# An attention and two expert layers on one core: float32r zero products, at changing addresses, in the idle places of the first batch

## The chip, the core and the metric

The kernel runs on one core of a Trainium2 chip, as one program in one launch. The metric is the device time of that core in microseconds (us). Five engines work side by side, each through its own queue of instructions: TensorE (PE) multiplies matrices, VectorE (DVE), ScalarE (ACT) and GpSimd (POOL) work on elements, and SyncE (SP) starts the transfers between the chip's memory and the core's.

## The reference

Three layers follow each other. The output of the attention is laid out as 4608 tokens of 512 values, and is the input of the first expert layer, whose output is the input of the second.

```python
def _attn_ref(q, k, v):                      # 8 batches, 8 heads, 576 positions, 64 values
    k_p = k.reshape(B, H, 72, 8, D).mean(axis=3)
    v_p = v.reshape(B, H, 72, 8, D).mean(axis=3)
    scores = scale * np.matmul(q, k_p.transpose(0, 1, 3, 2))
    scores = scores - np.max(scores, axis=-1, keepdims=True)
    attn = np.exp(scores)
    attn = attn / (np.sum(attn, axis=-1, keepdims=True) + 1e-09)
    return np.matmul(attn, v_p)

def _moe_ref(x, w_in, w_out):                # 4608 x 512, 512 x 2048, 2048 x 512
    h = x @ w_in
    return (h * np.cos(h)) @ w_out

def _moe2_ref(x, w_in, w_out):               # the same sizes
    h = x @ w_in
    return (h * np.clip(h + 3.0, 0.0, 6.0) / 6.0) @ w_out
```

## The kernel before

**The attention** goes batch by batch, and each batch in five query units of 128, 128, 128, 128 and 64 positions. `unit_s` (products at L490 or L494, all through `pe`) multiplies a unit's queries `qT` with the pooled keys, four heads a half; the keys stand block by block in `kbd`, a pair of tiles whose other places are zero. In batch 0 each half's maximum is taken on DVE (`mx`, L521) and the exponential on ACT with its sum (L531); in later batches DVE subtracts the maximum (`e`, L524) and ACT takes one exponential for the unit (L541). `unit_norm` turns the sum into a reciprocal on DVE (`sm`, L549 to L551), scales `e` with it on POOL (L553) and copies the rest of the heads aside (L555). `unit_pt` turns `e` over by products with the identity matrix `ident` and ACT copies the result to `pf` (L587); `unit_pt_rest` does that for the rest (L608). `pv` multiplies `pf` with the pooled values `vmf` and `vrf` into a 128 x 256 output. In batch 0 ACT copies that output, rounded to float32r, to `xh` (L641), and DVE subtracts `xh` from the output and keeps the difference in `xl` (L642): so the expert layer's input stands in two parts.

**Around it**: `pool_k` sums eight neighbouring key positions on DVE (`pk`, L428, two instructions), from `raw_k`, which SP loads; `pool_v` does that for the values (`vt`, L442, two instructions). `convert_weights` unpacks the expert weights from 64-bit words: its steps are L126, L130, L135 and L138 on DVE, squares and copies on ACT and a difference on POOL (L143, L144). `fill` (L500) puts four bf16 products with the identity ahead of the scores of batch 1 and six ahead of its first output product.

**The first expert layer** multiplies float32r parts: three products stand for one in full precision. The products with the first matrix have line L301 (output `h`), those with the second L344 (output `y`); between them lie the cosine on ACT and DVE. From the end of batch 0 on, expert steps and pieces of the attention alternate on PE until the attention's last batch. The second expert layer (L1021) follows at the end, by blocks of seven products in place of eight.

**What sets the order.** A scheduler with costs of its own puts each engine's instructions in a row, from the program in the order it was written. In batch 0 `front` (L712) writes PE's order by hand: each product that goes through `pe` is tied behind the one ahead of it (`issue_after`) while `in_order` is not empty. The other engines' orders, and PE's after `in_order.clear()`, are the scheduler's.

**The idle places.** `front` calls `keep_busy` (L703) eight times, with the counts of `KB` (L710). Its products multiply a part of `kbd[1]`, which is zero then and is read as bf16, with itself; 128 columns of it are the weights, 512 the moving operand. The result goes to `y2`, a tile in PSUM, and nothing reads it. The first count, 20, comes ahead of the first scores. This text calls the seven other calls groups 1 to 7. Group 1 stands between the second unit's scores and the third's, group 2 behind the third's, groups 3 to 5 around the second and third turning over and the fourth unit's scores, group 6 behind the third unit's turning over, and group 7 behind the fourth's. Then come the last output products of that part and the free order.

The outputs of `pv` in batch 0 use `y2` and `y3` in turn, in the same PSUM as the zero products: `piece("v")` takes `y2` for the first and third of four output products and `y3` for the second and fourth. An output must have been read by L641 and L642 before the next product that is written to its place starts.

Of the kernel before, what the change touches and what calls it, by code (L numbers as in the profile page):

```python
# [9 lines left out]
F32R = mybir.dt.float32r  # L10
# [14 lines left out]
def f(ap):  # L25
    return ap.bitcast(F32)
# [3 lines left out]
def tile_kernel(ctx, tc, q, k, v, wi1, wo1, wi2, wo2, ident_d, mask_d, out):  # L30
    nc = tc.nc
# [3 lines left out]
    P = 128  # L35
    N = 512
# [44 lines left out]
    pool_a = ctx.enter_context(tc.tile_pool(name="pool_a", bufs=1))  # L81
# [317 lines left out]
    def load_kv(b, nm):  # L399
        if nm == "v":  # L400
            src = v[b]
            pairs = src.rearrange("(j x) e -> x j e", x=2 * SP)
            for half in range(2):
                o = half * NP * VR
                nc.sync.dma_start(
                    out=raw_t[o : o + NP * VR, NP, :],
                    in_=src.rearrange("(j x) e -> j x e", x=2 * SP)[:, P:],
                )
            nc.sync.dma_start(out=raw_t[:, :NP, :], in_=pairs[:P])
            return  # L410
        nc.sync.dma_start(out=raw_k, in_=k[b])
# [75 lines left out]
    def pe(fn, *args, **kw):  # L487

        if not in_order:
            return fn(*args, **kw)  # L490
        with ExitStack() as order:
            if in_order[-1] is not None:
                order.enter_context(tc.issue_after(in_order[-1].ins))
            in_order.append(fn(*args, **kw))  # L494
# [48 lines left out]
    def unit_norm(n):  # L543
        w = UNITS[n % NU][1]
        e = ebuf[n % NE][:w, : H * SP].rearrange("p (h s) -> p h s", s=SP)
        sm = sums.pop(n, None)
        if sm is None:
            sm = ap.tile([P, H, 4], F32, tag="sm", name="sm", bufs=3)[:, :, 0:1]
            nc.vector.tensor_reduce(out=sm[:w, :, 0], in_=e, op=ALU.add, axis=AX.X)  # L549
        nc.vector.tensor_scalar(out=sm[:w], in0=sm[:w], scalar1=1e-9, scalar2=None, op0=ALU.add)  # L550
        nc.vector.reciprocal(out=sm[:w], in_=sm[:w])  # L551
        eng = nc.vector if n in ND else nc.gpsimd
        eng.tensor_tensor(out=e, in0=e, in1=sm[:w].to_broadcast([w, H, SP]), op=ALU.mult)  # L553
        e = ebuf[n % NE][:w]
        eng.tensor_copy(  # L555
            out=e[:, H * SP :].rearrange("p (t j x) -> p t j x", t=2, x=VR),
            in_=pairs_of(e)[:, :, P:].unsqueeze(1).to_broadcast([w, 2, NP, VR]),
        )
# [95 lines left out]
    def attention():  # L654
# [5 lines left out]
        for n in range(NU, units + 3):  # L660
# [21 lines left out]
            while finished < normed and n - finished >= 2:  # L682
# [12 lines left out]
                if qi == NU - 1:  # L695
                    done.append(qb)
                    if qb + 1 < B:
                        pool_v(qb + 1)
                        make_v(qb + 1)
                        if qb + 2 < B:  # L700
                            load_kv(qb + 2, "k")

    def keep_busy(n):  # L703

        z = kbd[1].rearrange("p j x -> p (j x)").bitcast(BF16)
        ps = ps_y.tile([P, N], F32, tag="y2", name="y2")
        for _ in range(n):
            pe(nc.tensor.matmul, ps, z[:, :P], z[:, :N], start=True, stop=True)

    KB = [20, 7, 9, 3, 4, 3, 3, 4]  # L710

    def front():  # L712

# [14 lines left out]
        w_convert(3)  # L728
        in_order.append(None)
        keep_busy(KB[0])  # L730

        def s(n):
            unit_s(n, 0)
            unit_s(n, 1)

        s(0)
        load_q(4)
        s(1)
        keep_busy(KB[1])
        unit_norm(0)  # L740
        s(2)
        unit_norm(1)
        keep_busy(KB[2])
        unit_pt(0)
        keep_busy(KB[3])
        s(3)
        pool_v(0)
        make_v(0)
        load_kv(1, "k")
        keep_busy(KB[4])  # L750
        unit_pt(1)
        unit_pt_rest(0, 0)
        unit_norm(2)
        w_convert(1)
        keep_busy(KB[5])
        for j in range(NP):
# [31 lines left out]
    for bl in range(NB):  # L788
        n = NAL[bl]
        steps += [(0, (0, bl), bl, fc, fc == 0, fc == n - 1) for fc in range(n)]  # L790
    SA = len(steps)
    for bl in range(NB):
        n = NAL[bl]
# [35 lines left out]
    def w_convert(n=3):  # L829
        nonlocal converted  # L830
        m, fc, hf, home = wjobs[converted]
        converted += 1
        running.extend(convert_weights(m, fc, hf))
        w_ops(n)
# [336 lines left out]
    for step, pb in enumerate(ORDER2):  # L1171
        t0, w = PAIRS[pb]
# [10 lines left out]
        for n in range(7):  # L1183
            for q in range(4):
                at = ring[turns2 % 3]
# [64 lines left out]
```

## Time and profile before

| | |
|---|---|
| median of three runs | 1657.24 us (1656.57 to 1657.41) |
| the profiled execution, its own time | 1657.06 us |
| its span, first to last instruction | 1655.3 us |
| mean granted clock of TensorE | 0.998 |
| busy: PE, DVE, ACT, POOL | 1635.6, 1107.3, 892.7, 313.4 us |
| share of the chain that ended last: PE, DVE, DMA, ACT | 94%, 3%, 1%, 1% |

The profile is that of one execution, and its times start at the first instruction. The time of a run is 1.76 us longer than the span. Busy times are sums over an engine's instructions, and say how full an engine is, not whether its time counts: for that one looks at a stretch, and at what ended each wait in it. PEclk is the clock that PE was granted, 1.00 for 2.4 GHz and 0.50 for 1.2 GHz; PEld are PE's weight loads, which run beside its products; DMA is the busy share of the 16 DMA engines and GB/s what they moved. A row of a timeline joins instructions of one kind that follow each other, and gives the start of the first. A float32r product is shown as f32 in the rows.

### The profile page before, as it was taken

The page shows a single profiled execution, that of the slowest core. Times are in us where ns is not written, and L with a number is a line of the kernel's source. Part 1 is how long each engine was busy: PE and PEld are TensorE (multiplying, and loading weights), DVE is VectorE, ACT ScalarE, POOL GpSimd, SP SyncE. Part 2 cuts the span into 40 slices and gives each one's busy share as a digit, 9 for nine tenths or more (in the row PEclk, how much of TensorE's full clock was granted, in tenths as well). Part 3 has the DMA queues.
Part 4 walks back from the last instruction along what each step waited for, and adds up shares of the span by engine and source line. Part 5 has one row for each costly group of instructions (what it writes and reads, how often), then busy time and mean ns, then how long its engine had stood idle before and what let it go on. Part 6 is the DMA issues. An engine that isn't in the chain of part 4 may idle for free.

```text
span 1655.3 us, 21211 instructions
## 1 busy us (share of the span) xinstructions
PE 1635.6 (99%) x7725; PEld 1343.0 (81%) x7727; DVE 1107.3 (67%) x1522; ACT 892.7 (54%) x1328; POOL 313.4 (19%) x257
## 2 busy tenths in 40 slices
PE   8999999999999999999999999999999999999999
PEld 4666788888888888888888898888878888888889
DVE  7998466665676778887776444545364676767665
ACT  6687687776555555555555333435353444444444
POOL 5466343232332111001114002022020000000000
PEclk9999999999999999999999999999999999999999
DMA  8687243124343575666653573242449944435130
GB/s 253 214 271 234 83 125 94 59 67 138 126 123 107 172 251 191 207 204 203 207 177 125 179 286 144 105 178 115 152 156 331 359 171 153 140 115 177 53 123 31
DMA packets 154760, 273.05 MB, mean 165 GB/s; under 512 B 16288, under 2 KB 79904, under 8 KB 153632
## 3 DMA queue, kind: packets, MB, share of 16 engines
q1 hardware_dynamic: 154656, 271.70, 49.1%
q8 instruction: 61, 1.00, 0.2%
q14 instruction: 43, 0.35, 0.1%
HBM read 166.79 MB, written 104.86 MB: 164 GB/s over the span
## 4 chain that ended last, share of the span: by engine, by line
PE 94%; DVE 3%; DMA 1%; issue 1%; ACT 1%; SPq 0%; POOL 0%; DVEq 0%; POOLq 0%; ACTq 0%
PE bank L1021 42%; PE h L301 23%; PE y L344 23%; PE ap_ps L490 6%; DMA raw_v<-in_v_dram 1%; DMA raw_k<-in_k_dram 1%; DVE pk L428 0%; DVE mx L521 0%; DVE vt L442 0%; DVE a L138 0%; PE ap_ps L500 0%; DVE e L524 0%; DVE a L126 0%; DVE sm L550 0%; DVE sm L549 0%
## 5 line engine op out<-in xcount | busy, mean ns | idle before, releaser
L1021 PE MATMUL bank<-wa,wb 128*128 128x512 f32 (+1 forms) x1368 | 287.7, 358 | 0.0
L1021 PEld LDWEIGHTS bank<-wa,wb 128*128 128x128 f32 x1368 | 231.2, 189 | 37.7
L344 PE MATMUL y<-gh,wb 128*128 128x512 f32 x648 | 210.9, 389 | 0.0
L301 PE MATMUL h<-xh,wb 128*128 128x512 f32 x648 | 206.6, 389 | 0.0
L883 ACT ACTIVATE wa<-wu 128x1024 fp32r<-128x1024 f32 (+1 forms) x130 | 127.3, 980 | 141.8 <-PE bank L1021 121.2
L1021 PE MATMUL bank<-wu,wb 128*128 128x512 f32 (+1 forms) x792 | 198.4, 386 | 0.0
L314 DVE SCALAR_TENSOR_TENSOR g<-h,t 128x512 f32<-128x512 f32 x144 | 99.1, 688 | 110.7 <-ACT t L309 110.0
L1021 PEld LDWEIGHTS bank<-wu,wb 128*128 128x128 f32 x792 | 148.8, 188 | 29.9
L344 PE MATMUL y<-gh,wa 128*128 128x512 f32 x504 | 170.0, 396 | 0.0
L301 PE MATMUL h<-xh,wa 128*128 128x512 f32 x504 | 165.8, 402 | 0.4 <-ACT xh L641 0.4
L275 POOL TENSOR_TENSOR xl<-xr,xh 128x512 fp32r<-128x512 f32 x68 | 94.9, 1412 | 325.9 <-ACT xh L274 277.8
L309 ACT ACTIVATE t<-h 128x512 int32<-128x512 f32 x144 | 85.4, 593 | 123.5 <-PE h L301 122.8
L317 ACT ACTIVATE g<-g,bias_c 128x512 f32<-128x512 f32 x144 | 104.2, 724 | 79.1 <-DVE g L314 78.3
L344 PEld LDWEIGHTS y<-gh,wb 128*128 128x128 f32 x648 | 121.7, 188 | 25.2
L301 PEld LDWEIGHTS h<-xh,wb 128*128 128x128 f32 x648 | 121.6, 188 | 25.2
L324 ACT ACTIVATE gh<-g 128x512 fp32r<-128x512 f32 x144 | 90.4, 628 | 68.1 <-DVE g L321 67.8
L884 DVE TENSOR_TENSOR wa<-wu,wa 128x1024 fp32r<-128x1024 f32 (+1 forms) x80 | 89.5, 1123 | 55.4 <-ACT wa L883 55.3
L344 PE MATMUL y<-gl,wb 128*128 128x512 f32 x324 | 126.0, 389 | 0.0
L301 PE MATMUL h<-xl,wb 128*128 128x512 f32 x324 | 122.6, 389 | 0.0
L321 DVE TENSOR_TENSOR g<-h,g 128x512 f32<-128x512 f32 x144 | 98.6, 685 | 32.4 <-ACT g L317 32.0
L1021 PE MATMUL bank<-wa,wa 128*128 128x512 f32 (+1 forms) x552 | 117.4, 359 | 0.0
L1139 ACT ACTIVATE wu<-bank,bias_c 128x1024 f32<-128x1024 f32 (+1 forms) x60 | 61.8, 1031 | 94.3 <-PE bank L1021 94.2
(176 smaller groups left out, 2873.9 us busy)
## 6 DMA issues: line engine op xcount, KB each, us to landing
g_d<-wu SPq DMA_DIRECT2D x64, 512.0 KB, 3.0
wu<-g_d SPq DMA_DIRECT2D x56, 512.0 KB, 4.4
wb<-s_d SPq DMA_DIRECT2D x36, 512.0 KB, 4.8
xr<-x_d SPq DMA_DIRECT2D x68, 256.0 KB, 3.3
s_d<-wa SPq DMA_DIRECT2D x32, 512.0 KB, 3.6
s_d<-wa SPq DMA_DIRECT2D x32, 384.0 KB, 3.0
raw_k<-in_k_dram SPq DMA_DIRECT2D x8, 1152.0 KB, 6.0
yp_d<-ys SPq DMA_DIRECT2D x36, 256.0 KB, 3.3
```

Of the source, the lines that this page charges most:

```text
L275: nc.gpsimd.tensor_tensor(out=xl, in0=t, in1=f(xh), op=ALU.subtract)
L301: nc.tensor.matmul(h, (wh, wl)[a][:, cs], xs_[key, c][z], start=(n == 0), stop=(n == 3 * NC - 1))
L309: nc.scalar.activation(out=t, in_=hs[s], func=AF.Copy, bias=0.25, scale=INV_2PI)
L314: mark[s] = nc.vector.scalar_tensor_tensor(out=g, in0=hs[s], scalar=INV_2PI, in1=t, op0=ALU.mult, op1=ALU.subtract)
L317: nc.scalar.activation(out=g, in_=g, func=AF.Sin, scale=TWO_PI, bias=bias_c[:, 1:2])
L321: nc.vector.tensor_tensor(out=g, in0=hs[s], in1=g, op=ALU.mult)
L324: nc.scalar.activation(out=gh, in_=g, func=AF.Copy)
L344: nc.tensor.matmul(y[c], a, z, start=(first and n == 0), stop=(last and n == 2))
L490: return fn(*args, **kw)
L883: nc.scalar.activation(out=hi, in_=src, func=AF.Copy)
L884: el.tensor_tensor(out=lo, in0=src, in1=f(hi), op=ALU.subtract)
L1021: nc.tensor.matmul(bank[:, e, :wide], w[:, j, h, e], z[:, j], start=start and j == 0 and x == 0, stop=stop and j == 1 and x == 2, skip_gro ...
```

## The change

The first 20 zero products stay as they are. Those of groups 1 to 7 read a tile of their own, `zeros`, which takes the slot `a13` of pool_a (a slot that holds weights later) and is set to zero by one instruction on POOL. They are float32r, and go through a list of 14 pairs of offsets, three products at each pair: the first number moves the moving operand, the second the weights, in elements of four bytes, so the two addresses take different values modulo 256 bytes. The counts of groups 1 to 7 go from 7, 9, 3, 4, 3, 3, 4 to 9, 9, 6, 3, 3, 6, 6, which is 33 before and 42 after. The lines behind the new code stand 17 further down.

```diff
@@ -700,14 +700,31 @@
                         if qb + 2 < B:
                             load_kv(qb + 2, "k")
 
+    PLACES = [
+        (0, 0), (0, 32), (0, 16), (0, 48), (32, 32), (32, 0), (16, 16),
+        (16, 0), (0, 8), (0, 56), (8, 8), (32, 48), (48, 48), (48, 32),
+    ]
+    zeros = pool_a.tile([P, 1024], F32R, tag="a13", name="wa13", bufs=1)
+    nc.gpsimd.memset(f(zeros), 0.0)
+    zeroed = []
+
     def keep_busy(n):
 
         z = kbd[1].rearrange("p j x -> p (j x)").bitcast(BF16)
         ps = ps_y.tile([P, N], F32, tag="y2", name="y2")
         for _ in range(n):
-            pe(nc.tensor.matmul, ps, z[:, :P], z[:, :N], start=True, stop=True)
-
-    KB = [20, 7, 9, 3, 4, 3, 3, 4]
+            zeroed.append(n)
+            if len(zeroed) <= KB[0]:
+                pe(nc.tensor.matmul, ps, z[:, :P], z[:, :N], start=True, stop=True)
+                continue
+            at, w = PLACES[(len(zeroed) - KB[0] - 1) // 3]
+            w += N
+            pe(
+                nc.tensor.matmul, ps, zeros[:, w : w + P], zeros[:, at : at + N],
+                start=True, stop=True,
+            )
+
+    KB = [20, 9, 9, 6, 3, 3, 6, 6]
 
     def front():
 
```

The scheduler counts the new products at costs of its own, and so writes other orders on all engines: on DVE, ACT and POOL in the stretch up to some 150 to 240 us, on PE up to some 600 us. From there on each engine's order is the same as before. Two places show what moves.

On DVE, in batch 0, around the first four output products of `pv`, before the change (`xl` is L642's difference of an output `y2` or `y3`, `pk` the keys' sum for batch 1, `sm` the fifth unit's sum, `a` and `e` belong to a weight's conversion; numbers behind a name tell tiles apart):

```order
L138 SCALAR_TENSOR_TENSOR a_313<-e_314,a_313 128x512
L642 TENSOR_TENSOR xl_326<-y2_322,xh_325 128x256
L428 TENSOR_REDUCE pk_425<-raw_k_107 128x144
L642 TENSOR_TENSOR xl_333<-y3_329,xh_332 128x256
L428 TENSOR_REDUCE pk_425<-raw_k_107 128x144
L642 TENSOR_TENSOR xl_340<-y2_336,xh_339 128x256
L550 TENSOR_SCALAR sm_411<-sm_411 64x8
L642 TENSOR_TENSOR xl_347<-y3_343,xh_346 128x256
L551 RECIPROCAL sm_411<-sm_411 64x8
L135 SCALAR_TENSOR_TENSOR a_477<-st_148,a_477 128x512
```

The same place after the change:

```order
L138 SCALAR_TENSOR_TENSOR a_319<-e_320,a_319 128x512
L428 TENSOR_REDUCE pk_436<-raw_k_107 128x144
L642 TENSOR_TENSOR xl_332<-y2_328,xh_331 128x256
L642 TENSOR_TENSOR xl_339<-y3_335,xh_338 128x256
L428 TENSOR_REDUCE pk_436<-raw_k_107 128x144
L550 TENSOR_SCALAR sm_422<-sm_422 64x8
L135 SCALAR_TENSOR_TENSOR a_488<-st_150,a_488 128x512
L642 TENSOR_TENSOR xl_346<-y2_342,xh_345 128x256
L642 TENSOR_TENSOR xl_353<-y3_349,xh_352 128x256
```

The first sum `pk` now stands ahead of the first subtraction and the second subtraction ahead of the second sum; L550 and L135, which stood behind the third subtraction, stand ahead of it. The third subtraction (from `y2`) is the one that must have read `y2` before group 6 may write there.

On PE, around the first turning over in batch 1, which started at 58.42 us before the change (`ident,e_104` and `ident,e_105` are the turnings over of its first and second unit, `kbd,qT` a unit's scores; rows of L301 and L344 are products of an expert step with the first and second matrix; the rows left out are four `fill` products):

```order
L344 MATMUL y_909<-gh,wa_138 128x512
L301 MATMUL h<-xh,wa_752 128x512 x4
L301 MATMUL h<-xl,wa_752 128x512 x4
L301 MATMUL h<-xh,wa_753 128x512
L490 MATMUL ap_ps<-ident,e_104 128x128 x4
...
L490 MATMUL ap_ps<-kbd_102,qT 128x144 x4
L301 MATMUL h<-xh,wa_753 128x512 x3
L490 MATMUL ap_ps<-ident,e_105 128x128 x4
```

The same place after the change (behind the second "..." six more rows of L344 are left out, and the last of the eight stands):

```order
L301 MATMUL h<-xl,wa_763 128x512
L301 MATMUL h<-xh,wa_764 128x512 x4
L344 MATMUL y_917<-gh,wa_139 128x512
L344 MATMUL y_917<-gl,wa_139 128x512
L344 MATMUL y_917<-gh,wa_140 128x512
L490 MATMUL ap_ps<-ident,e_104 128x128 x4
...
L490 MATMUL ap_ps<-kbd_102,qT 128x144 x4
L344 MATMUL y_918<-gh,wa_139 128x512
...
L344 MATMUL y_920<-gl,wa_139 128x512
L490 MATMUL ap_ps<-ident,e_105 128x128 x4
```

Three products of the second matrix stand ahead of that turning over in place of one with the first, and eight of the second matrix in place of three of the first ahead of the next one. The `fill` products that stood behind the second turning over still stand there.

## Rows read from the trace of the kernel before

**Rows 1.** Stretches: length, busy PE, PEld, DVE, ACT, POOL (instructions), PEclk, DMA, GB/s.

```profile
64.30:67.70 3.40, 2.94 (x12) 2.07 (x11) 3.40 (x6) 3.37 (x6) 2.12 (x2) 0.50 0.92 359
67.70:139.00 71.30, 70.71 (x326) 48.47 (x326) 65.72 (x111) 53.19 (x94) 42.64 (x39) 1.00 0.76 246
142.80:146.20 3.40, 3.40 (x11) 2.85 (x11) 1.47 (x3) 3.37 (x6) 2.52 (x3) 0.50 0.83 238
160.00:1655.30 1495.30, 1489.29 (x7037) 1242.45 (x7035) 967.54 (x1281) 775.87 (x1066) 224.24 (x167) 1.00 0.47 157
```

**Rows 2.** PE's timeline, 0 to 60 us: start, length, instructions, [idle before <- releaser].

```profile
11.29 1.67 PE L494 MATMUL y<-kbd 128*128 128x512 bf16 x7
12.80 0.65 PE L494 MATMUL ap_ps<-kbd,qT 128*128 128x144 f32 x4
14.34 0.76 PE L494 MATMUL h<-kbd,qT 128*128 128x144 f32 x4 [0.88 <-ACT e L531]
...
22.19 0.88 PE L494 MATMUL y<-ident,e 128*128 128x128 f32 x6 [1.66 <-POOL e L553]
...
31.46 0.81 PE L494 MATMUL y<-kbd 128*128 128x512 bf16 x2
...
34.03 0.33 PE L490 MATMUL y<-ident,e 64*128 64x64 f32 x2 [0.25 <-POOL e L553]
...
37.44 0.50 PE L301 MATMUL h<-xh,wa 128*128 128x512 f32 x1 [0.38 <-ACT xh L641]
37.77 0.41 PE L490 MATMUL ap_ps<-kbd,qT 128*128 128x144 f32 x2
```

**Rows 3.** PE's timeline, products of the first matrix in a row.

```profile
55.10 1.07 PE L301 MATMUL h<-xh,wa 128*128 128x512 f32 x4
56.01 1.07 PE L301 MATMUL h<-xl,wa 128*128 128x512 f32 x4
```

**Rows 4.** DVE's timeline, 25 to 35 us.

```profile
27.06 0.67 DVE L138 SCALAR_TENSOR_TENSOR a<-e,a 128x512 f32<-128x512 bf16 x1
...
27.99 1.33 DVE L428 TENSOR_REDUCE pk<-raw_k 128x144 f32<-128x1152 f32 x1
...
30.84 0.40 DVE L642 TENSOR_TENSOR xl<-y,xh 128x256 fp32r<-128x256 f32 x1
31.17 0.57 DVE L550 TENSOR_SCALAR sm<-sm 64x8 f32<-64x8 f32 x1
31.66 0.41 DVE L642 TENSOR_TENSOR xl<-y,xh 128x256 fp32r<-128x256 f32 x1
...
32.10 0.86 DVE L135 SCALAR_TENSOR_TENSOR a<-st,a 128x512 uint32<-128x512 uint32 x1
```

**Rows 5.** PE's timeline, the scores and turnings over behind batch 0.

```profile
51.19 0.65 PE L490 MATMUL ap_ps<-kbd,qT 128*128 128x144 f32 x4
...
58.42 0.66 PE L490 MATMUL ap_ps<-ident,e 128*128 128x128 f32 x4 [1.12 <-POOL e L553]
...
64.76 1.01 PE L500 MATMUL ap_ps<-ident 128*128 128x256 bf16 x4 [2.39 <-ACT pf L587]
...
141.57 0.63 PE L490 MATMUL ap_ps<-ident,e 128*128 128x128 f32 x4 [2.09 <-DVE e L524]
```

**Rows 6.** DVE's timeline, 56 to 107 us.

```profile
56.93 0.19 DVE L551 RECIPROCAL sm<-sm 128x8 f32<-128x8 f32 x1
...
69.56 0.18 DVE L551 RECIPROCAL sm<-sm 128x8 f32<-128x8 f32 x1
...
71.81 1.74 DVE L442 TENSOR_REDUCE vt<-raw_v 128x192 f32<-128x1536 f32 x1
...
106.53 1.35 DVE L428 TENSOR_REDUCE pk<-raw_k 128x144 f32<-128x1152 f32 x1 [2.05 <-DMA raw_k<-in_k_dram]
```

**Rows 7.** ACT's timeline, 62 to 65 us.

```profile
62.25 1.28 ACT L541 ACT_TABLE_LOAD   x1
...
64.13 0.58 ACT L587 ACTIVATE pf<-ap_ps 128x512 f32<-128x512 f32 x1
```

## The prediction

> **What bounds the kernel now.** I read the table by stretches first, to see which engine fills which part. From 160 us to the end TensorE (PE) is busy for 1489.29 of 1495.30 us [rows 1], and the change leaves every instruction there where it was; so the end comes as early as PE enters that part, and what PE loses or wins before 160 us goes through one to one. Second, the clock column of the same table: PE is granted half its clock in 64.3 to 67.7 us and in 142.8 to 146.2 us [rows 1], each time behind a wait of PE of more than 2 us (2.39 us before 64.76, 2.09 us before 141.57 [rows 5]). Half the clock over 3.4 us loses about 1.7 us of PE's work each time. Third, PE's timeline, for its waits and what the zero products cost. Fourth, VectorE's (DVE's): between 67.7 and 139 us it is busy for 65.72 of 71.30 us while PE is busy for 70.71 [rows 1]; here both are nearly full, and DVE has as much say as PE.
>
> **The zero products.** A bf16 product of 512 columns costs 0.216 us: seven take from 11.29 to 12.80 [rows 2]. Where float32r products follow each other, four take from 55.10 to 56.01, 0.227 us each [rows 3]. The first of a run costs more, because its weights are not loaded behind the work ahead: the one at 37.44 keeps the next back until 37.77, 0.33 us, so 0.11 us is exposed [rows 2]. A group of n then costs 0.227n + 0.11 us in place of 0.216n. The seven groups go from 7, 9, 3, 4, 3, 3, 4 (33 products, 7.1 us) to 9, 9, 6, 3, 3, 6, 6: 42 x 0.227 + 7 x 0.11 = 10.3 us, or 3.2 us more. Bounds: no row shows other pairs of addresses. Below, 0.216 (the bf16 row) would give 9.1 us; above, the dearest I can read is 0.33 for every one, 13.9 us. I take 0.227, the nearest row in type and size, and keep -1.2 and +3.6 us for the range. The measured 0.227 is what enters the sum. The Trainium skill's page "TensorE: Matmul & The Clock Gate", section "Back-to-back issue gap", gives one gap for 512 columns whatever the type, 518 cycles, some 0.216 us; by it the 42 products would be 0.5 us cheaper. The rows agree with that for bf16 and not for float32r.
>
> Most of this lies in time in which PE waited anyway. Group 1 grows by 0.64 us ahead of a wait of 0.88 us (14.34), groups 3 to 5 together by about 0.9 us around one of 1.66 us (22.19) [rows 2]: no cost, and if those covers were gone, 1.5 us. The memset of the operand is one instruction on GpSimd before anything waits for that engine: no cost.
>
> **The wait that the change adds.** Groups 6 and 7 do not hide. Group 6 writes y2, which must first be read by the xl subtraction (L642) of the third output product of this batch. In DVE's old order that is reached at 30.84 us, after xl, pk, xl, pk [rows 4]. In the new one the same four rows stand ahead of it in another order, and then L550 and L135 as well. By their lengths of 0.57 and 0.86 us, less the 0.08 us by which a row reaches into the next (31.17 to 31.66), it starts 1.2 us later, at about 32.1, and ends near 32.5. The group stood at about 31.46 before; it starts 1.0 us later, is 0.8 us longer, and group 7 is 0.6 us longer: 2.4 us. The waits of 0.25 us (34.03) and 0.38 us (37.44) [rows 2] go, so the first expert product comes about 1.8 us late, at 39.2 us. Behind it are queued all of PE's later instructions, and DVE's row maxima wait for those.
>
> **The order behind it.** Now the order matters more than the products. Before the transposes that start at 58.42 us PE used to run 33 products of the first matrix and 12 of the second; now 36 and 3, six fewer, 1.4 us. The fourth unit's scores stand behind ten more of them, 2.3 us. So PE, 1.8 us late, ends those scores near 51.7 + 1.8 + 2.1 = 55.6 us (51.7 is the old end; 0.2 us of exposed loads goes). The reciprocal of the first unit, which came at 56.93 [rows 6], now stands directly behind that unit's maximum and no longer behind the second pk: about 56.2. GpSimd's scaling takes the same 1.5 us from there as between 56.93 and 58.42: e is there at 57.7, when PE has just run five and three products more (55.6 + 1.9 = 57.5). The wait of 1.12 us [rows 5] shrinks to about 0.2.
>
> Next stands the wait of 2.39 us for pf [rows 5]. ScalarE came to pf at 64.13 behind a table load of 1.28 us at 62.25 and an exponential [rows 7]. It has the same two ahead of it now, but its earlier work ends sooner, since three expert steps no longer alternate in between; counted through, pf starts at about 62.4 and ends at 63.0. PE meanwhile runs eight products of the second matrix in place of three of the first and gets there at 62.3. So the four fillers start at about 63.05, not 64.76, with the same 48 expert products done: **PE is 1.7 us ahead**, the 3.2 us included. And these two waits are about 1 us together in place of 3.5, so I expect no drop of the clock there: another 1.7 us, **3.4 us in all at 68 us**.
>
> **What is late next.** DVE. At the reciprocal that stood at 69.56 us [rows 6] it would be 4.2 us early, of which 2.2 us is work put off (a vt reduction, a maximum, two subtractions): 2.0 us ahead. By the wait at 141.57 us one L138 more (0.67 us at 27.06, 0.6 without the reach into the next [rows 4]) stands behind and not ahead: 2.6 us. PE, 3.4 us ahead, then waits 0.8 us longer there, its clock falls a second time as before, and what remains is DVE's lead. **The sum: 1657.06 us (the profiled execution: its span of 1655.30 and 1.76 us around it; the median of the runs is 1657.24) - 2.6 = 1654.5 us.** The unknown product price, -1.2 to +3.6 us, is half hidden by the longer waits: about -0.6 to +1.8 on this.
>
> **Rivals.**
> 1. *More than I count.* DVE waited 2.05 us for raw_k at 106.53 [rows 6]. In the new order that load stands earlier in SP's queue, and DVE has 20 rows between the two pk pairs there, more than before. If that wait goes too, DVE is 4.6 us ahead at 141.57, PE waits about 1 us and keeps its clock: 2.6 + 2.0 + 1.7 = 6.3, **1650.8 us**. Against it: PE's products would have to be in step everywhere between.
> 2. *Slower.* In the new order both pk reductions of batch 4 (1.3 us each by the row at 27.99 [rows 4]), the longer vt reduction (1.66 us by the next start; 1.74 at 71.81 [rows 6]) and an L321 (about 0.6) stand ahead of the reciprocal that stood near 100 us: 4.8 us more work ahead of it. Against the lead of 2.0 us that unit comes 2.8 us later than before; PE, which is early, waits there, and its clock falls once more (1.7 us): +4.5, **1661.6 us**. It decides if DVE still stands at pk for raw_k, so that rival 1's 2 us are not won, and if PE has no other products ahead of those transposes.
> 3. *No gain.* The 1.8 us from batch 0 run through: the waits of 1.12 and 2.39 us are set by DVE's and ScalarE's chain, and if that starts as late as PE does, PE waits as long as before and its clock falls in the same two places. The change then adds zero products and nothing else: **1657.1 us**, up to 1658.9 if none of the 1.8 us hides.
>
> **How the numbers follow.** Forecast 0.45, rival 1 0.25, rival 2 0.15, rival 3 0.15. A measurement of this kernel can tell about 0.2% (3.3 us) from no change, so faster means under 1653.9 us and slower over 1660.6. The forecast's own range, 1652.5 to 1656.5, lies on both sides of the first bound: a third of it is faster. Faster 0.25 + 0.14 = 0.39, slower 0.14 (rival 2, of which a little falls short of the bound), the rest 0.47 is within. For 8 in 10 the range must hold the forecast, rival 3, most of rival 1 and the near part of rival 2: 1650.5 to 1660.0 us.
>
> **What would show it.** Right: float32r zero products 0.227 us apart with 0.11 us before the second; group 6 starting at 32 to 33 us behind xl; the first expert product at 39 us; the four fillers of 64.76 at about 63; no half clock near 64 us; a longer wait of PE near 137 us. Wrong: products at some addresses clearly over 0.24 us; pf no earlier than 64 us; a stretch of half clock anywhere between 40 and 130 us; PE waiting for e near 100 us. What I trust least is the count through DVE's and ScalarE's new order over 100 us, where one wait more moves the end by its length.

## The result, and the profile after

| | before | after | ratio, 95% interval |
|---|---|---|---|
| with the result | 1657.33 us, 4 runs | 1667.09 us (1664.75 to 1672.38), 4 runs | 1.0062 [1.005, 1.0074] |
| once more | 1657.82 us, 15 runs | 1665.0 us (1663.98 to 1669.63), 5 runs | 1.0046 [1.0032, 1.0059] |

The change makes the kernel about 0.5% slower, 7 to 10 us. The forecast was 1654.5 us in a range up to 1660.0, so the time lies outside it and on the other side.

The profiled execution took 1672.38 us, the slowest of its four runs. Two rows of its table by stretches, with the columns of [rows 1]:

```profile
40.00:57.00 17.00, 15.37 (x47) 11.16 (x46) 10.75 (x17) 4.57 (x10) 5.99 (x6) 0.60 0.46 149
...
160.00:1670.60 1510.60, 1504.44 (x7102) 1254.49 (x7101) 979.37 (x1301) 788.14 (x1083) 230.55 (x174) 1.00 0.47 157
```

From 160 us on PE is as full as before (idle for 6.2 us, against 6.0), so the loss lies ahead of that. The prediction's sentence that every instruction there stays where it was is too strong, since PE's order differs up to some 600 us; it does no harm to the sum. What is new is the clock: 0.60 in 40 to 57 us, where PE was at full clock before. Its PE timeline, with the columns of [rows 2]:

```profile
10.92 2.34 PE L494 MATMUL y<-wa 128*128 128x512 f32 x9
13.10 0.65 PE L494 MATMUL ap_ps<-kbd,qT 128*128 128x144 f32 x4
...
22.49 1.33 PE L494 MATMUL y<-ident,e 128*128 128x128 f32 x6 [1.94 <-POOL e L553]
...
42.02 0.70 PE L494 MATMUL y<-pf,vmf 128*128 128x256 f32 x2 [1.63 <-DVE xl L642]
```

The clock is half in 22.7 to 26.2, 43.2 to 56.9, 77.4 to 80.8 and 159.3 to 162.7 us, 23.9 us in all, against 6.8 before. On the page PE is busy for 1647.2 us in place of 1635.6 and idle for 23.4 in place of 19.7. So the 15.3 us between the two profiled executions are (23.9 - 6.8) / 2 = about 8.5 us of half clock, 3.2 us of zero products (the prediction's count) and 3.7 us of waits.

Most of the 8.5 us belongs to that execution: the four runs have mean granted clocks of 0.993, 0.998, 0.997 and 0.996 in the order of 1672.38, 1664.75, 1665.81 and 1668.36 us. A second profile of the same kernel (1665.0 us, clock 0.998 as before) has half clock for 6.8 us like before, and is the one to compare. PE's waits in it:

```profile
22.46 0.88 PE L494 MATMUL y<-ident,e 128*128 128x128 f32 x6 [1.94 <-POOL e L553]
...
29.22 0.70 PE L494 MATMUL y<-pf,vmf 128*128 128x256 f32 x2 [1.10 <-DVE xl L642]
...
32.14 1.64 PE L494 MATMUL y<-wa 128*128 128x512 f32 x6
...
38.71 0.50 PE L301 MATMUL h<-xh,wa 128*128 128x512 f32 x1
...
40.38 0.70 PE L494 MATMUL y<-pf,vmf 128*128 128x256 f32 x2 [0.93 <-DVE xl L642]
...
64.82 0.60 PE L500 MATMUL ap_ps<-ident 128*128 128x256 bf16 x4 [1.02 <-ACT pf L587]
...
69.42 0.63 PE L490 MATMUL ap_ps<-ident,e 128*128 128x128 f32 x4 [1.72 <-DVE e L524]
```
```profile
97.67 1.20 PE L301 MATMUL h<-xh,wa 128*128 128x512 f32 x4 [1.00 <-ACT wa L143]
...
106.37 0.97 PE L344 MATMUL y<-gh,wa 128*128 128x512 f32 x3 [0.71 <-ACT gh L324]
...
116.46 0.50 PE L301 MATMUL h<-xl,wa 128*128 128x512 f32 x1 [0.83 <-POOL xl L275]
...
146.16 0.63 PE L490 MATMUL ap_ps<-ident,e 128*128 128x128 f32 x4 [1.49 <-DVE e L524]
...
151.73 1.19 PE L490 MATMUL ap_ps<-kbd,qT 128*128 128x144 f32 x4 [2.48 <-DVE e L524]
```

Here PE is busy for 1639.8 us of 1663.2, so idle for 23.4 us. Of the 7.9 us that this span is longer, 3.7 are waits, 3.2 the products, and 1.0 is other time in which PE counts as busy. This tells what PE did and not what caused it: the crossed kernels below part that.

### The profile page after: what moved, and what is told of

Read it like the earlier page. It is cut to its first block, busy times and chain, and to the rows that moved or that the text cites. A ratio compares the mean times of both kernels' runs of the same rounds, so it can differ in the third digit from the quotient of the medians.

```text
span 1670.6 us, 21235 instructions
## 1 busy us (share of the span) xinstructions
PE 1647.2 (99%) x7736; PEld 1352.7 (81%) x7736; DVE 1113.2 (67%) x1522; ACT 891.1 (53%) x1326; POOL 312.8 (19%) x258
## 4 chain that ended last, share of the span: by engine, by line
PE 92%; DVE 4%; issue 1%; POOL 1%; ACT 1%; DMA 1%; SPq 0%; POOLq 0%; DVEq 0%; ACTq 0%
PE bank L1038 41%; PE h L301 22%; PE y L344 22%; PE ap_ps L490 5%; DMA raw_v<-in_v_dram 1%; DVE a L138 1%; PE y L494 1%; POOL e L553 0%; DVE mx L521 0%; DVE vt L442 0%; DVE a L130 0%; DVE a L126 0%; DVE sm L549 0%; POOL xl L275 0%; DVE e L524 0%
## 5 line engine op out<-in xcount | busy, mean ns | idle before, releaser
L1038 PEld LDWEIGHTS bank<-wa,wb 128*128 128x128 f32 x1368 | 231.2, 189 | 37.6
L344 PE MATMUL y<-gh,wb 128*128 128x512 f32 x648 | 210.8, 389 | 0.0
L301 PE MATMUL h<-xh,wb 128*128 128x512 f32 x648 | 206.6, 389 | 0.0
L344 PE MATMUL y<-gh,wa 128*128 128x512 f32 x504 | 171.9, 399 | 0.7 <-ACT gh L324 0.7
L301 PE MATMUL h<-xh,wa 128*128 128x512 f32 x504 | 166.1, 405 | 1.1 <-ACT wa L143 1.0
L275 POOL TENSOR_TENSOR xl<-xr,xh 128x512 fp32r<-128x512 f32 x68 | 95.1, 1416 | 321.9 <-ACT xh L274 274.6
L301 PEld LDWEIGHTS h<-xh,wb 128*128 128x128 f32 x648 | 121.7, 188 | 25.2
L344 PEld LDWEIGHTS y<-gh,wb 128*128 128x128 f32 x648 | 121.6, 188 | 25.1
L344 PE MATMUL y<-gl,wb 128*128 128x512 f32 x324 | 126.0, 389 | 0.0
L301 PE MATMUL h<-xl,wb 128*128 128x512 f32 x324 | 122.7, 389 | 0.0
L321 DVE TENSOR_TENSOR g<-h,g 128x512 f32<-128x512 f32 x144 | 98.5, 684 | 33.3 <-ACT g L317 32.7
L301 PEld LDWEIGHTS h<-xh,wa 128*128 128x128 f32 x504 | 94.8, 191 | 22.6 <-issue 2.3
```

The costliest lines, as they stand in the source:

```text
L275: nc.gpsimd.tensor_tensor(out=xl, in0=t, in1=f(xh), op=ALU.subtract)
L301: nc.tensor.matmul(h, (wh, wl)[a][:, cs], xs_[key, c][z], start=(n == 0), stop=(n == 3 * NC - 1))
L321: nc.vector.tensor_tensor(out=g, in0=hs[s], in1=g, op=ALU.mult)
L344: nc.tensor.matmul(y[c], a, z, start=(first and n == 0), stop=(last and n == 2))
L1038: nc.tensor.matmul(bank[:, e, :wide], w[:, j, h, e], z[:, j], start=start and j == 0 and x == 0, stop=stop and j == 1 and x == 2, skip_gro ...
```

## What was tried

The theory after the result was **order**: the new counts make the scheduler write other orders, and these make the waits. The rivals were **type** (float32r products hold the clock less well than bf16 ones), **address** (some of the 14 pairs are slow) and **products** (9 more of them make the other engines late).

Each number below is the median of 4 to 11 runs. Its ratio is to the kernel before, run beside it.

### Type and addresses

`after_again` is the second profile of the changed kernel told of above.

> The changed kernel once more, to see how its runs spread and to have a second profile. The profiled execution took 1672.38 us, with half the clock in 23.4 to 26.7, 43.3 to 56.8, 77.4 to 80.9 and 159.6 to 163.0 us. Theory clock-by-chance (the long stretch of half clock differs from run to run, the waits do not): median 1664 to 1668 us, runs spread by over 4 us, a run's time less half its time at half clock the same within 1 us. Rival (the long stretch belongs to this kernel in every run): all runs above 1664, the stretch of 13.5 us in the new profile too.

The theory's median and spread came true (1665.0 us, 5.7 us apart), and the stretch of 13.5 us is not in the new profile. The two profiled executions, less half of their time at half clock, are 1660.4 and 1661.6 us, 1.2 us apart.

Three kernels change one property each. The scheduler's orders turned out to depend on the counts alone: with the new counts the rows of DVE, ACT, POOL and PE in the trace stand as in the changed kernel, with the old ones DVE's and PE's as before (ACT has two rows moved by two places, POOL the one that sets `zeros`).

```diff
 bf16_after
+            zz = zeros.bitcast(BF16)
-                nc.tensor.matmul, ps, zeros[:, w : w + P], zeros[:, at : at + N],
+                nc.tensor.matmul, ps, zz[:, 2 * w : 2 * w + P], zz[:, 2 * at : 2 * at + N],
 f32r_oldcounts
-    KB = [20, 9, 9, 6, 3, 3, 6, 6]
+    KB = [20, 7, 9, 3, 4, 3, 3, 4]
 oneplace
+    PLACES = [(0, 0)] * 14
```

> The changed kernel with its 42 zero products as bf16 ones, from the same tile at the same byte offsets; every engine's order is that of the changed kernel. Theory order (the new counts move the order, and the order makes the waits; the type has no part): the products get 42 x 0.015 + 7 x 0.095 = 1.3 us shorter, the waits of 1.63 us for xl near 42 us and 1.94 us for e near 22 us stay or grow, the time is 1663 to 1667 us, still over 0.3% slower than before. Rival type (float32r products hold the clock less well than bf16 ones): the clock does not fall near 23 and 43 us and the time comes to 1655 to 1661 us.

> The changed kernel with the counts of before (33 zero products, float32r, the same pairs of addresses); DVE's order is that of before. Theory order: 33 x 0.015 + 7 x 0.095 = 1.2 us more zero products, half of it hidden in waits: 1657 to 1659 us, half clock at 64 and 142 us as before. Rival type: the clock falls near 22 or 43 us too, 1660 to 1668 us with a spread of some us.

> The changed kernel with all 42 float32r zero products at the first pair of addresses (0, 0); the order is that of the changed kernel. Theory order: the addresses have no part, products 0.227 to 0.235 us apart, the same median as the changed kernel within 2 us. Rival address (some pairs are slower or hold the clock less well): products nearer to 0.227 us, fewer stretches of half clock, 3 us or more faster than the changed kernel.

| kernel | counts, order | products | median | ratio, interval |
|---|---|---|---|---|
| after_again | new | float32r, 14 pairs | 1665.0 us | 1.0046 [1.0032, 1.0059] |
| bf16_after | new | bf16 | 1665.04 us | 1.0038 [1.0026, 1.0051] |
| oneplace | new | float32r, 1 pair | 1665.36 us | 1.0047 [1.0035, 1.006] |
| f32r_oldcounts | old | float32r, 14 pairs | 1658.31 us | 1.0002 [0.9994, 1.0011] |

Type and address fall. With the old counts float32r at all those addresses costs nothing that can be measured; with the new ones bf16 from the same byte offsets is as slow. At full clock the float32r products of a run are 0.22 to 0.24 us apart in every profile, with one pair of addresses as with 14, and the second of a run comes 0.31 to 0.34 us behind the first. The clock near 23 us doesn't tell the types apart either: it fell in the profiles of `bf16_after` and `oneplace`, and not in that of `after_again`.

### Order or products

To part the two, a table ties each engine's rows behind each other in a given order, over the whole stretch in which the two orders differ (the zero products stay where `pe` puts them). So each order can be run with each count.

```diff
+ORDER = {"DVE": [0, 1, 2, ...], "Activation": [...], "Pool": [...], "SP": [...], "PE": [...]}
+    for engine, order in ORDER.items():
+        for x, y in zip(order, order[1:]):
+            tc.add_manual_dep(rows[engine][y], rows[engine][x].name, info, reason="order")
```

> The changed kernel, its 42 float32r zero products included, with every engine's order that of the kernel before (tied row by row behind each other). It differs from the kernel with the old counts only by 9 products, 9 x 0.231 = 2.1 us of TensorE. Theory order (what costs is where the scheduler puts the other engines' instructions): 1658 to 1661 us, the wait of 2.39 us for pf near 66 us as before, no wait for weights near 100 us. Rival products (the added products make the other engines late): 1663 to 1667 us.

> The changed kernel with the counts of before (33 float32r zero products) and every engine's order that of the changed kernel. Theory order: 1662 to 1666 us, with the changed kernel's waits: about 1 us for the weights wa, 0.7 us for gh and 0.8 us for xl between 95 and 120 us, and two for e of 1.5 and 2.5 us near 150 us. Rival products: 1657 to 1660 us, without these waits.

| float32r products | order of before | order of the changed kernel |
|---|---|---|
| 33 (old counts) | 1658.31 us, 1.0002 [0.9994, 1.0011] | 1665.12 us, 1.0042 [1.0028, 1.0055] |
| 42 (new counts) | 1659.27 us, 1.0009 [1.0001, 1.0018] | 1665.0 us, 1.0046 [1.0032, 1.0059] |

The two crossed kernels have their order tied, the other two have it from the scheduler. The order costs 6.8 us with the old counts and 5.7 us with the new ones. The nine products and the ties, which no run parts, come to about 1 us together with the order of before. PE's waits in the two crossed kernels go with the order, and not with the count. First the order of before with 42 products, then the new order with 33:

```profile
65.99 0.67 PE L500 MATMUL ap_ps<-ident 128*128 128x256 bf16 x4 [2.39 <-ACT pf L587]
...
144.62 0.85 PE L490 MATMUL ap_ps<-ident,e 128*128 128x128 f32 x4 [2.09 <-DVE e L524]
```
```profile
98.76 1.20 PE L301 MATMUL h<-xh,wa 128*128 128x512 f32 x4 [1.06 <-ACT wa L143]
...
152.81 0.73 PE L490 MATMUL ap_ps<-kbd,qT 128*128 128x144 f32 x4 [2.49 <-DVE e L524]
```

### What in the order costs the time

DVE runs the same rows in both orders. Grouped by line, the four steps of the weights' conversion up to about 160 us (DVE's; count, then busy us and mean ns of one, then idle time before them), in the kernel before and in `after_again`:

```profile
L135 DVE SCALAR_TENSOR_TENSOR a<-st,a 128x512 uint32<-128x512 uint32 x14 | 13.7, 978 | 0.1
L130 DVE SCALAR_TENSOR_TENSOR a<-st,a 128x512 uint32<-128x512 uint32 x14 | 13.4, 957 | 0.0
...
L138 DVE SCALAR_TENSOR_TENSOR a<-e,a 128x512 f32<-128x512 bf16 x14 | 10.9, 777 | 0.0
...
L126 DVE TENSOR_SCALAR a<-st 128x512 uint32<-128x512 uint32 x14 | 9.6, 686 | 2.1 <-POOL wa L144 1.4 <-DMA st<-in_moe_w_in_dram 0.7
```
```profile
L130 DVE SCALAR_TENSOR_TENSOR a<-st,a 128x512 uint32<-128x512 uint32 x14 | 15.1, 1079 | 0.2
L138 DVE SCALAR_TENSOR_TENSOR a<-e,a 128x512 f32<-128x512 bf16 x14 | 15.0, 1070 | 0.3 <-ACT e L125 0.3
...
L126 DVE TENSOR_SCALAR a<-st 128x512 uint32<-128x512 uint32 x14 | 12.1, 868 | 2.7 <-POOL wa L144 2.1 <-DMA st<-in_moe_w_in_dram 0.7
L135 DVE SCALAR_TENSOR_TENSOR a<-st,a 128x512 uint32<-128x512 uint32 x14 | 10.7, 767 | 0.0
```

They are 14 rows each, 47.6 us before (13.7 + 13.4 + 10.9 + 9.6) and 52.9 us after (15.1 + 15.0 + 12.1 + 10.7): the same 56 rows take 5.3 us longer, 3.1 of them in one row of L138. `old_order_new_counts` has 48.1 us and `new_order_old_counts` 51.9, so this goes with the order too. Single rows show why. DVE and POOL of `after_again` near the last wait:

```profile
146.96 3.76 DVE L138 SCALAR_TENSOR_TENSOR a<-e,a 128x512 f32<-128x512 bf16 x1
150.64 0.45 DVE L521 TENSOR_REDUCE mx<-ap_ps 128x4 f32<-128x288 f32 x1
151.12 0.46 DVE L524 TENSOR_TENSOR e<-ap_ps,mx 128x288 f32<-128x288 f32 x1
```
```profile
146.42 2.52 POOL L275 TENSOR_TENSOR xl<-xr,xh 128x512 fp32r<-128x512 f32 x2
148.91 1.26 POOL L330 TENSOR_TENSOR gl<-g,gh 128x512 fp32r<-128x512 f32 x1
```

L138 takes 3.76 us where POOL runs three instructions back to back beside it (two L275, one L330), and 0.68 us where POOL is idle, in the kernel before:

```profile
137.40 0.68 DVE L138 SCALAR_TENSOR_TENSOR a<-e,a 128x512 f32<-128x512 bf16 x1
```

Behind the long one stand the maximum L521 and the subtraction L524, and for L524 PE waited 2.48 us before 151.73. All rows that last over 0.25 us more than the shortest of their kind, 24 before and 25 after, are of these four lines, of L550 or (one, before) of L456, and have POOL at work beside them; L428, L442, L521 and L524 never stretch. POOL beside a row is needed and not enough: of the 56 rows, 38 before and 40 after have it beside them for over 0.2 us, and 18 and 21 of these stretch; of the others none does. The Trainium skill's page "SBUF — State Buffer", section "Who interferes with whom", says that DVE and GpSimd share a pair of ports, that an instruction of DVE with two SBUF inputs contends there with one of GpSimd that reads SBUF, that in a mode that uses both ports whoever issues first has the pair for the whole instruction while the other waits, and that reductions on trn2 never contend. The trace agrees, down to L428 and L442 (reductions) keeping their 1.34 and 1.73 us.

Two kernels move single rows of DVE's table. The first puts the second vt reduction behind two xl subtractions, since in the changed kernel's own profile DVE ran it ahead of them and PE waited 1.63 us before 42.02:

```profile
39.89 1.74 DVE L442 TENSOR_REDUCE vt<-raw_v 128x192 f32<-128x1536 f32 x1
41.55 0.74 DVE L642 TENSOR_TENSOR xl<-y,xh 128x256 fp32r<-128x256 f32 x2
```

```diff
 new_order_xl_first, DVE
-    ..., 55, 58, 56, 59, 38, 39, 57, ...
+    ..., 55, 58, 56, 38, 39, 59, 57, ...
 new_order_L138_behind, DVE
-    ..., 186, 192, 255, 198, 199, ...
+    ..., 186, 192, 198, 199, 255, ...
```

> The changed kernel, its order tied, but for one row: the second vt reduction (1.74 us on DVE), which stands ahead of two xl subtractions near 40 us, goes behind them, as it stood before the change. It should take away TensorE's wait for xl (1.63 and 0.93 us in two profiles). If that wait is passed on to the end: 1 to 1.6 us off the changed kernel, 1663 to 1664.5 us. If the chain through DVE and the later waits set the time anyway: within 0.5 us of the changed kernel's 1665 to 1667 us.

1665.48 us, 1.0042 [1.0028, 1.0055]. The wait for xl was gone, and one of 0.51 us (for xh, before 43.85) came. The fillers started at 65.13 us, against 65.63 in `oneplace`, whose profile has the same half clock near 23 us, so half of the wait came off there. At the end no gain can be seen, as the rival says, though the interval is too wide to rule out the theory's 1 us.

> The changed kernel, order tied, with one DVE row moved: the L138 that took 3.76 us at 146.96 us, beside three GpSimd instructions, goes behind the maximum and the subtraction (L521, L524) for which TensorE waited 2.48 us at 151.73. Theory (a row that runs beside GpSimd is stretched, and what is queued behind it makes TensorE wait): that wait falls under 0.7 us, 1.5 to 2.5 us off the changed kernel's 1665 to 1667, 1 to 2 us more where the clock no longer falls behind it: 1661 to 1664 us. Rival (another wait takes its place at once): within 0.7 us of the changed kernel.

1662.56 us, 1.0028 [1.0016, 1.0041]: 2.4 us under the changed kernel's 1665.0, in the theory's range, but the two intervals overlap, so the size is not shown. That the wait goes is. On DVE and PE:

```profile
155.73 0.46 DVE L524 TENSOR_TENSOR e<-ap_ps,mx 128x288 f32<-128x288 f32 x1
156.11 1.96 DVE L138 SCALAR_TENSOR_TENSOR a<-e,a 128x512 f32<-128x512 bf16 x1
```
```profile
153.49 0.63 PE L490 MATMUL ap_ps<-ident,e 128*128 128x128 f32 x4 [1.50 <-DVE e L524]
...
159.75 0.41 PE L490 MATMUL ap_ps<-ident,e 128*128 128x128 f32 x2 [0.62 <-DVE sm L551]
...
162.86 1.19 PE L490 MATMUL ap_ps<-kbd,qT 128*64 128x144 f32 x8
```

In `after_again` the last of these products stands at:

```profile
159.00 1.19 PE L490 MATMUL ap_ps<-kbd,qT 128*64 128x144 f32 x8
```

L138 still lasts 1.96 us beside POOL, but L524 is through ahead of it. PE no longer waits for it; its next wait there is 0.62 us, for another row. From the turning over to the scores of the fifth unit PE takes 9.37 us (153.49 to 162.86) in place of 12.84 (146.16 to 159.00). Of these 3.5 us 1.9 are the wait (2.48 less 0.62), and about 1.7 the half clock that stands in 151.8 to 155.3 us of `after_again` and nowhere there in this profile. So one stretched row with the wrong rows behind it costs 1.9 us of waiting of the 6 to 7 us, and 3.5 in this pair of profiles, where the clock fell behind it.

Three more kernels were to show where the rest lies.

```diff
 new_order_pk_behind, with the row of new_order_L138_behind; DVE, then ACT
-    ..., 129, 148, 130, 132, 134, 137, 135, 138, 136, 139, ...
+    ..., 129, 130, 132, 134, 137, 135, 138, 136, 148, 139, ...
-    ..., 121, 128, 120, 116, 125, 126, 129, 122, 123, ...
+    ..., 121, 120, 116, 125, 126, 122, 128, 129, 123, ...
```

> The changed kernel, order tied, L138 moved as in the run before (1662.56 us), and besides the second pk reduction of batch 3 (1.33 us on DVE at 89.31 us) put behind the weights' L138 at 95.85, with the two copies that need it put behind the weights' copy L143 on ACT. TensorE waited 1.00 us for that copy (wa) at 97.67. Theory (what stands ahead of the weights on DVE makes them late, and the waits for e, gh and xl behind it follow from that): the wait for wa falls under 0.3 us, 1 to 2.5 us come off, 1660 to 1661.6 us. Rival (each of those waits has its own row, the next takes over, or the keys are late instead): 1662 to 1665 us.

1672.96 us, 1.0093 [1.0075, 1.011]. The wait for wa stayed, and two others grew, for e and for xs:

```profile
98.97 1.20 PE L301 MATMUL h<-xh,wa 128*128 128x512 f32 x4 [0.99 <-ACT wa L143]
103.43 0.73 PE L490 MATMUL ap_ps<-kbd,qT 128*128 128x144 f32 x4 [2.14 <-DVE e L524]
...
106.84 1.12 PE L490 MATMUL ap_ps<-ident,e 128*128 128x128 f32 x4 [2.68 <-ACT xs L646]
```

This is over both ranges. The moved row came late to what needs it: ACT's second copy of the keys to `kbd` started at 99.54 us in place of 94.83, and the subtraction L524 behind the moved row at 102.84 in place of 99.57. That is nearest to the rival's last case, and the test does not say what the weights' lateness costs.

```diff
 old_then_new; new_then_old has the two the other way round
+    n = {"DVE": 121, "PE": 244, "Activation": 111, "Pool": 42, "SP": 75}
+    ORDER[engine] = BEFORE[engine][:n[engine]] + CHANGED[engine][n[engine]:]
```

> The changed kernel (42 float32r zero products), every engine's order tied: up to about 75 us the order of before, from there that of the changed kernel. Theory late rows (the new order costs its time on DVE between 75 and 155 us, where more of DVE's rows run beside GpSimd's and are stretched): 1663 to 1666 us, DVE's stretched rows 4 us or more above those of the kernel with the order of before throughout (16.5 us). Rival front (it is lost in the first batch): 1659 to 1661 us.

> The other half: up to about 75 us the changed kernel's order, from there that of before. Theory late rows: 1659 to 1661 us. Rival front: 1663 to 1666 us.

1676.95 us, 1.0117 [1.0102, 1.0133], and 1682.97 us, 1.0163 [1.0145, 1.0181]: both halves are slower than either whole, with waits of 10.21 us for e (before 117.32) and of 4.96 us for xh (before 129.14) that neither whole order has. The seam itself costs more than what was to be measured, so their times decide nothing. Their other waits do say where each belongs. With the order of before up to 75 us, PE still waits 1.27 us for wa, 0.71 for gh, 0.87 for xl, and 1.49 and 2.47 for e; with the new order up to 75 us and that of before behind it, it waits 1.03 us for pf and 1.71 for e near 70 us, and none for wa, gh or POOL's xl. So the late waits come with the order from 75 us on.

### The other orders and counts

```diff
 old_order_vt_behind, DVE
-    ..., 256, 255, 257, 185, 189, 191, 190, 186, 192, ...
+    ..., 256, 255, 185, 189, 191, 190, 257, 186, 192, ...
```

> The kernel with the old counts in float32r (1658.31 us), order of before tied, with one DVE row moved: the second vt reduction near 138 us (1.74 us) goes behind the maxima and the subtraction for which TensorE waited 2.09 us at 142. The same theory on the old order: that wait falls to about 0.4 us and 1 to 3 us come off: 1655.5 to 1657.5 us, which is under both kernels. Rival (the values that vt makes are then late, or the next wait takes over): 1657.5 to 1660 us.

1660.44 us, 1.0016 [1.0007, 1.0025]; no gain. On DVE and PE:

```profile
140.91 1.74 DVE L442 TENSOR_REDUCE vt<-raw_v 128x192 f32<-128x1536 f32 x1
144.32 0.69 DVE L321 TENSOR_TENSOR g<-h,g 128x512 f32<-128x512 f32 x1 [1.67 <-ACT g L317]
```
```profile
145.48 0.73 PE L490 MATMUL ap_ps<-kbd,qT 128*128 128x144 f32 x4 [3.24 <-issue]
```

The subtraction did come earlier. But ACT has a copy that needs vt ahead of the sine that L321 waits for, so DVE stood 1.67 us for ACT. For PE's 3.24 us the view names no releaser; the subtraction L524 behind L321 ends at 145.38 us, just ahead of the end of that wait. A row that is moved on one engine must be moved on those that wait for it.

> The kernel before, its order tied, without the zero products of groups 6 and 7 (7 bf16 products, 1.5 us of TensorE ahead of the first expert product). Theory order says that the other engines' rows set the time from 40 us on: 1656.5 to 1658.5 us. If TensorE's own time counted: 1655 to 1656.5 us. If the emptier stretch lets the clock fall near 40 us: 1658.5 to 1660 us.

> The order of before tied, only the first 20 zero products left and none in groups 1 to 7. Without groups 6 and 7 it took 1661.52 us, with half the clock for 20 us from 36 us in its profile. If the zero products are there for the clock, and idle places without them let it fall: 1662 to 1670 us, half clock in the first 60 us in the profile. If their 7 to 8 us of TensorE were only in the way: 1655 to 1658 us.

```diff
 old_order_g67none
+    KB = [20, 7, 9, 3, 4, 3, 0, 0]
 old_order_none
+    KB = [20, 0, 0, 0, 0, 0, 0, 0]
```

1661.52 us, 1.0026 [1.0016, 1.0035], and 1670.01 us, 1.007 [1.0057, 1.0084]. Taking 33 products away makes the kernel 12.6 us slower than the one before (1657.45 us beside it). Two rows of its table by stretches:

```profile
13.60:28.10 14.50, 10.18 (x38) 7.74 (x38) 11.68 (x24) 10.98 (x60) 7.39 (x8) 0.53 0.77 240
...
37.40:58.60 21.20, 21.20 (x60) 14.39 (x59) 7.82 (x15) 5.55 (x12) 6.68 (x8) 0.52 0.37 122
```

The clock is down for 34 of the first 59 us. The mean granted clocks of its six runs are 0.986 to 0.992, those of the kernel before beside it 0.997 to 0.999: by an estimate from these means, some 16 us more of PE's work are lost, which is over the 12.6. So the zero products earn their time by the clock; groups 6 and 7, 1.5 us of PE, are worth 3.7 us (1661.52 against 1657.83). The kernel before stays the fastest of all that ran.

## Why the prediction was wrong, step by step

| step | before | forecast | measured (`after_again`) |
|---|---|---|---|
| a group of 9 float32r products | - | 2.15 us | 2.18 us (10.92 to 13.10, first profile) |
| group 6 starts | 31.46 | 32.5 | 32.14 us |
| first expert product | 37.44 | 39.2 | 38.71 us |
| fillers behind the 48th expert product | 64.76 | 63.05 | 64.82 us |
| wait near 141.57 ends | 141.57 | 139.0 | 146.16 us |
| time of the profiled execution | 1657.06 | 1654.5 | 1665.0 us |

**The products** were right: 0.23 us each and some 0.1 us more for the first, no pair over 0.24. The front came in nearly as counted, group 6 and the first expert product being at most 0.5 us off, but this was luck in part: the wait behind it was another. The prediction had group 6 wait for the third xl subtraction, to end near 32.5 us. That subtraction was through in time, and no wait stands before group 6 at 32.14:

```profile
31.42 0.41 DVE L642 TENSOR_TENSOR xl<-y,xh 128x256 fp32r<-128x256 f32 x1
```

What PE waited for was the first xl, which now stands behind a pk sum: 1.10 us before the third output product at 29.22, where the kernel before had 0.42 (and 0.26 before the fourth, where the changed kernel has none):

```profile
28.12 0.70 PE L494 MATMUL y<-pf,vmf 128*128 128x256 f32 x2 [0.42 <-DVE xl L642]
```

**The order behind it** is the first step that failed. "The four fillers start at about 63.05" rested on pf ending at 63.0, counted through ACT's rows. PE's wait there shrank, as counted (1.02 us, 0.75 forecast), but it ended at 64.82: its end had not moved. The count of DVE's order stopped at the third xl. It did not see that behind it the second vt reduction had come ahead of two xl subtractions, at which PE stood 0.93 us before 40.38. Taking it away moved the fillers by 0.5 us, so it is the smaller part of the 1.8 us. The rest lies in the chain to pf, as rival 3 said. The scores that the prediction has end at 55.6 us (it calls them the fourth unit's; by their count they are the third's) only start at 56.40, and ACT, which waited 0.49 us for a product of PE, then works without a gap up to pf, with two table loads of 1.28 us among its rows:

```profile
58.31 0.60 ACT L309 ACTIVATE t<-h 128x512 int32<-128x512 f32 x1 [0.49 <-PE h L301]
...
64.19 0.58 ACT L587 ACTIVATE pf<-ap_ps 128x512 f32<-128x512 f32 x1
```

So pf starts at 64.19 us and not at 62.4, with 64.13 before the change.

**The clock.** "No drop of the clock there" was right at 64 us, but behind the next wait (1.72 us for e, before 69.42) it fell at 69.9 us, so the 1.7 us were not won.

**What is late next** is the term with the largest error, -2.6 us forecast and +4.6 measured at the same wait. From the fillers to that wait, in the kernel before and in `after_again`, with the columns of [rows 1]:

```profile
64.80:141.57 76.77, 74.09 (x338) 50.58 (x338) 71.19 (x120) 58.43 (x102) 47.33 (x42) 0.98 0.76 246
```
```profile
64.80:146.16 81.36, 74.81 (x334) 49.52 (x333) 73.69 (x119) 54.92 (x98) 46.27 (x42) 0.98 0.72 233
```

PE is idle 3.9 us longer there. DVE is busy 2.5 us longer, with one row fewer, and idle 2.1 us longer; its waits for PE's scores come to 4.0 us in place of 1.3. DVE's lead was summed from its rows' lengths in the trace of before. The four rows of 1.00 to 1.76 us that start between 91 and 96 us in `after_again`, the last of them the L138 for which ACT's copy of wa and then PE waited, are not lengths that such a row keeps when it is moved: they go with what POOL does at that moment. Of the 5.3 us by which the four lines' rows grew, some 2 lie ahead of this wait, and 3.1 in the L138 of 3.76 us, which starts at 146.96, behind it. From the wait to the end 3.3 us more were lost, and the largest wait in them is the one of 2.48 us behind that L138.

**The rivals.** Rival 1's condition came true without its gain: of DVE's two waits for raw_k up to 165 us (6.3 us) one is left (4.0), but what was won there went again in longer waits for PE's scores and for `wa` (1.4 to 2.1). Rival 2 had the side and the place right: pk reductions ahead of DVE's other work, PE waiting from 97 us on, though for the weights and not for a unit's e. Its 1661.6 us left out the stretching and lay 3.4 to 5.5 us short. With a chance of 0.15 it stood outside the range, whose upper end was 1660.0.

**What stays open**: of the 6 to 7 us that the order costs, 1.9 us of waiting are shown to hang on L138; the half clock behind that wait is there in one profile and not in the other, which alone does not show that it hangs on it. That the rest follows from the stretched rows between 85 and 120 us (waits of 1.00 for wa, 0.71 for gh, 0.83 for xl) is argued and not shown: no run took these waits away alone.

## What to carry to other kernels

When an edit only feeds a scheduler other counts, measure the order apart from the edit: tie each engine's rows to the old order and run the new work in it, and the reverse. A forecast that walks a new order with old row lengths holds as far as no row changes neighbours; for rows of the kinds that stretched here, look first at what GpSimd will be doing beside them. And a filler's price is not its time: look at what the clock does without it.

## What the runs showed of the chip

**The same wait lowers the clock in one run and not in the next.** The wait of 1.94 us at 22.5 us was followed by half clock in the changed kernel's first profile and not in its second. The wait of 2.09 us near 142 us, behind which the clock fell in the kernel before, left it up in `f32r_oldcounts`:

```profile
142.89 0.63 PE L490 MATMUL ap_ps<-ident,e 128*128 128x128 f32 x4 [2.09 <-DVE e L524]
```
```profile
142.30:149.00 6.70, 5.49 (x32) 4.21 (x33) 4.42 (x11) 5.85 (x11) 5.26 (x6) 1.00 0.71 213
```

So one profile's clock column, on which the forecast's two losses of 1.7 us rested, is one draw. But the draws are not alike in the two orders: with the new order in the first batch the clock fell before 40 us in 8 of 9 profiles, and with the order of before and its 33 or more zero products in none of 5. So a part of what the order costs may be clock; that was not parted. The Trainium skill's page "TensorE: Matmul & The Clock Gate", section "Part 1: The HAM clock gate (the "warmup" mystery)", says that the chip's window runs free of the kernel and that one kernel measures differently from run to run; these pairs agree.

**Once down, the clock can stay down while PE is fully busy.** It came back after 3.4 us in most places, but after 13.6 us from 43.2 us in the changed kernel's first profile, where PE was busy all the while, and after 20.5 us from 37.6 us in `old_order_none`, PE busy for 21.20 of 21.20 us in the row above. What PE ran there were the end of batch 0 and the first expert step, in pieces of 64 to 512 columns. What of it keeps the clock down was not tried.
